# Two heads over two adjacent PSUM banks in one instruction, in the attention steps of a gated mix of two attention blocks

## The chip, the cores and the metric

One core of a Trainium2 chip runs the kernel as one program. The time is device microseconds of one launch. Three runs of the kernel before gave 2834.82 to 2836.29 us, median 2835.33. The engines are called PE (TensorE, matrix products), ACT (ScalarE, activations), DVE (VectorE, reductions and element-wise work), POOL (GpSimd) and SP (SyncE, which issues most DMAs). Each runs its own instructions in the order in which they were written, and semaphores order the engines among each other.

## The reference

Two multi-head attention blocks, A and B, each with its own weights, read the same input `x` of 2048 rows and 640 features (the reference gives `A_x` to both). Each has 32 heads of 20 features. A sigmoid gate of `x` mixes the two results row by row.

```python
q, k, v = qkv[0], qkv[1], qkv[2]
scores = jnp.einsum("bhqd,bhkd->bhqk", q, k) * scale
p = _softmax(scores, axis=-1)
o = jnp.einsum("bhqk,bhkd->bhqd", p, v)
...
g = _sigmoid((x * gate_w).sum(-1, keepdims=True))
return g * a + (1 - g) * b
```

The softmax subtracts the largest score of each row, so the kernel computes every score twice: once to find the row maxima, and once more, transposed and with the maximum already subtracted, to take the exponential.

## The kernel before

The 64 heads of both blocks are taken in 16 groups of four, and the 2048 queries in four blocks of 512. For each group and query block there are eight steps of 256 keys, 512 steps in all (`STEPS`). The main loop (L1103) walks through them, and one step holds four kinds of work on PE:

- **Scores** (`scores`, L624): for each of the two key tiles and each of the two head pairs, two matmuls, 128 keys by 512 queries. The two heads of a pair stand on the two halves of PE's rows, at 0 and 64, and can run at the same time. Each lands in a PSUM bank, and ACT takes its exponential into an SBUF tile `pt` (L635). That is eight a step.
- **Values** (`values`, L645): four matmuls per key tile, of the step before, which add to the one PSUM bank `acc`. PE shows eight matmul records for each such block.
- **Maxima** (`max_mm`, L558): the scores of later steps, 128 queries by 512 keys, about 15 steps ahead (`LEAD`). A unit has four chunks of 512 keys, taken in the order 0, 2, 1, 3 (`ORDER`), and two heads. Chunks 2 and 3 of both heads, and for most groups chunks 0 and 1 of the second head, go through a plain row maximum on DVE (L585). For the first head, chunk 0 holds the difference of two chunks' keys (`KD`); ACT takes its positive part into `rl` (L578), and DVE adds that to chunk 1 and takes the maximum in one instruction (L582). In group 0 both heads do so.
- **Blocks that fill** (`slot`, L1053): projections of queries, keys and values for later groups, and output products. One block is some 6 to 15 matmuls into one bank (`mms`, L368), which ACT or DVE then empties.

PSUM has eight banks: one is `acc`, and the other seven (`NB`) are single tiles that `take` (L122) hands out. It picks the bank that a small cost model of the engines thinks will come free first. `T_EXP`, `T_MAX` and the like are that model's costs; they only set which bank is picked. PE cannot write a bank before the instruction that reads it has ended.

The order of a step's work is written out by hand in `STEP` (L44). A letter stands for one call: `e0` and `e1` the score matmul of the one or the other head, `m0` and `m1` that of the maxima, `V` a block of value products, `X` a filling block. There are three orders: for a step with no filling block, with one, and with two; `LATE` is for the last steps, in which no maxima are left. Beside the `e` calls the loop moves smaller pieces along: `take_acc` (L732), which transposes `acc` on DVE once in eight steps (L736, L741, L747), and `finish_max` (L589), which gathers the maxima and sends them through DRAM into the rows of `QT`.

Of the kernel before, what the change touches and what calls it, by code (L numbers as in the profile page):

```python
# [19 lines left out]
P = 128  # L20
# [3 lines left out]
DH = 20  # L24
# [28 lines left out]
T_EXP, T_MAX, T_BACK = 0.478, 0.6, 0.15  # L53
REST = 6
# [7 lines left out]
def kernel(  # L62
# [18 lines left out]
    psum = ctx.enter_context(tc.tile_pool(name="psum", bufs=1, space=PSUM))  # L81
# [18 lines left out]
    acc = psum.tile([P, QB], F32, name="acc")  # L100
# [21 lines left out]
    def take():  # L122

        i = min((k for k in range(NB) if k not in held), key=lambda k: free_at[k])
        held.add(i)
        return i, banks[i]

# [32 lines left out]
    def scales(maxima, n, then):  # L160

        for _ in range(REST):
            yield
        yield PRODUCT
        i, pt = take()
        nc.tensor.transpose(pt[:n, :P], maxima[:, :n], ident)
        tick_block(0.1, free_at[i])
        yield
        e = wts.tile([5, 8], F32, name="e", tag="scl", bufs=2)
        nc.vector.tensor_reduce(e[:n, 0:1], pt[:n, :P], axis=AX.X, op=OP.max)  # L170
        give(i, spend("dve", 0.3, clock["done"]))
        spend("dve", 1.0)
        powers(e.bitcast(I32)[:n, :], 1)
        dg = wts.tile([5, 2, 5], F32, name="dg", tag="scd", bufs=2)
        for k in range(2):
            nc.vector.tensor_scalar(dg[:n, k, :n], ident[:n, :n], e[:n, 3 + k:4 + k], None, op0=OP.mult)
        for _ in range(REST):
            yield
        yield PRODUCT
        i, pb = take()  # L180
        tick_block(0.1, free_at[i])
        for k in range(2):
            nc.tensor.matmul(pb[:, k * n:(k + 1) * n], ones[:n, :], dg[:n, k, :n], start=True, stop=True)  # L183
        yield
        both = wts.tile([P, 10], F32, name="both", tag="scb", bufs=2)
        nc.vector.tensor_copy(both[:, :2 * n], pb[:, :2 * n])
        give(i, spend("dve", 0.2, clock["done"]))
        then(both[:, :n], both[:, n:2 * n])
# [179 lines left out]
    def mms(i, out_ap, pairs, cost):  # L368

        if now[0] >= 0:  # L370
            tick_block(len(pairs) * cost * T_SCORE, free_at[i])
        for k, (a, b) in enumerate(pairs):
            if now[0] < 0:
                tick_block(cost * T_SCORE, free_at[i])
            nc.tensor.matmul(out_ap, a, b, start=(k == 0), stop=(k == len(pairs) - 1))  # L375
            if now[0] < 0:
                yield
# [6 lines left out]
    def project_chunk(w, hi, lo, ch):  # L384

        wh, wl = w
        def pairs(n):
            if now[0] < 0:
                return ([(wh[:, c, :], b[:, c, n]) for c in range(NC) for b in (xh, xl)]
                        + [(wl[:, c, :], xh[:, c, n]) for c in range(NC)])  # L390
            return [(a[:, c, :], b[:, c, n]) for c in range(NC) for a, b in ((wh, xh), (wh, xl), (wl, xh))]

        t0 = ch * QB
        if now[0] >= 0:
            f = work.tile([P, QB], F32, name="fs")
            for k in range(3):
                if k:
                    yield
                m = slice(PARTS[k], PARTS[k + 1])
                i, pt = take()  # L400
                yield from mms(i, pt[:, m], pairs(slice(t0 + m.start, t0 + m.stop)), 0.34)
                nc.scalar.activation(f[:, m], pt[:, m], AF.Copy, scale=QKS)  # L402
# [116 lines left out]
    def project_v(gg, j):  # L519
# [3 lines left out]
        for u in range(2):  # L523
            if u and now[0] >= 0:
# [5 lines left out]
            nc.scalar.activation(V[gg % 2][:, j + u, :, 0:DH], pt[:, :160].rearrange("p (h d) -> p h d", h=2 * GH),  # L530
                                 AF.Copy, scale=QKS)
# [20 lines left out]
    relus, relu_at = {}, {}  # L552
# [5 lines left out]
    def max_mm(u, ch, heads=(0, 1)):  # L558
# [9 lines left out]
        for j in heads:  # L568
            two = u < NS or ch < 2 and (j == 0 or g == 0)
# [3 lines left out]
            k = KD[g % 2 if ch == 0 else 1][r, pair] if two and ch % 2 == 0 else KT[g % 2][r, pair, ch * QB:(ch + 1) * QB]  # L573
            nc.tensor.matmul(pt, QT[g % 2][r, pair, q0:q0 + P], k, start=True, stop=True)  # L574
            m = mparts[g, qb][:, pair, j, t, ch:ch + 1]
            if two and ch % 2 == 0:
                relus[u, j] = start.tile([P, QB], F32, name="rl0", bufs=4) if u < NS else work.tile([P, QB], F32, name="rl", bufs=2)
                nc.scalar.activation(relus[u, j], pt, AF.Relu)  # L578
                back = relu_at[u, j] = spend("act", T_EXP, ready)
            elif two:  # L580
                rl = relus.pop((u, j))
                nc.vector.tensor_tensor_reduce(rl, pt, rl, 1.0, LOW, OP.add, OP.max, m)  # L582
                back = spend("dve", T_MAX, max(ready, relu_at.pop((u, j))))
            else:
                nc.vector.tensor_reduce(m, pt, axis=AX.X, op=OP.max)  # L585
                back = spend("dve", T_MAX, ready)
            give(i, back)

# [35 lines left out]
    def scores(G, kk, pair, heads=(0, 1)):  # L624
# [3 lines left out]
        for j in heads:  # L628
            i, et = take()
            ready = tick_score(j, i)  # L630
            r = slice(64 * j, 64 * j + 64)
            nc.tensor.matmul(et, KT[g % 2][r, pair, kt * P:(kt + 1) * P],  # L632
                             QT[g % 2][r, pair, qb * QB:(qb + 1) * QB], start=True, stop=True)
            pt = pp.tile([P, QB], F32, name="pt")
            nc.scalar.activation(pt, et, AF.Exp, scale=factor(g // 4))  # L635
# [9 lines left out]
    def values(G, kk):  # L645
# [3 lines left out]
        for h in range(GH):  # L649
            nc.tensor.matmul(acc[32 * h:32 * h + VW, :], V[(g // 2) % 2][:, kt, (g % 2) * GH + h, :],  # L650
                             ptiles.pop((G, kk, h)), start=(kt == 0), stop=(kt == NT - 1))
# [33 lines left out]
    def out_tiles(job, t, state):  # L685
# [17 lines left out]
        def products():  # L703
            wh, wl = wo_parts[z]
            for k in range(0, D, width):
# [8 lines left out]
                if first:  # L714
                    nc.scalar.activation(y[:, n], pt[:, :width], AF.Copy, scale=f)
                else:
                    nc.vector.scalar_tensor_tensor(y[:, n], pt[:, :width], f, y[:, n], op0=OP.mult, op1=OP.add)
# [52 lines left out]
    def take_last():  # L770
# [5 lines left out]
        for t in range(4):  # L776
            nc.tensor.matmul(pt[:, 4 * t:4 * t + 4], ot[:, t * P:(t + 1) * P], one, start=True, stop=True)
        rc = work.tile([P, 16], F32, name="sq", bufs=2)
        nc.vector.reciprocal(rc, pt[:, :16])
        give(i, spend("dve", 0.3))  # L780
        i, pt = take()
        nc.tensor.transpose(pt[:16, :P], rc, ident)
        rt = wts.tile([16, P], F32, name="rt", tag="rt", bufs=1)
        nc.scalar.activation(rt, pt[:16, :P], AF.Copy)
        give(i, spend("act", 0.3))
        i, pt = take()
        for t in range(4):
            nc.tensor.matmul(pt[:, t * P:(t + 1) * P], picks[0].rearrange("p k e -> p (k e)")[:, t * P:(t + 1) * P], rt,
                             start=True, stop=True)
        o = work.tile([P, 2, QB], F16, name="on", bufs=2)  # L790
        for t in range(4):
            c = slice(t * P, (t + 1) * P)
            nc.vector.tensor_tensor(ot[:, c], ot[:, c], pt[:, c], op=OP.mult)
# [8 lines left out]
    def last_tiles(qb, o):  # L802
        wh, wl = wo_parts[2]
        for t in range(4):
            c = slice(t * P, (t + 1) * P)
            f = f_o[1][:, 4 * qb + t:4 * qb + t + 1]
            for half in range(2):
# [4 lines left out]
                for k, (a, w) in enumerate(((0, wh), (0, wl), (1, wh))):  # L812
                    nc.tensor.matmul(pt[:, :320], o[:, a, c], w[:, n], start=(k == 0), stop=(k == 2))  # L813
                if half and qb == NQ - 1 and t < 3:
                    part = pp.tile([P, QB], F32, name="pt")[:, :320]
                    nc.scalar.activation(part, pt[:, :320], AF.Copy, scale=f)
                    nc.gpsimd.tensor_tensor(y, y, part, op=OP.add)
                    give(i, spend("act", 0.42, clock["done"]))
                else:
                    nc.vector.scalar_tensor_tensor(y, pt[:, :320], f, y, op0=OP.mult, op1=OP.add)  # L820
# [35 lines left out]
    def turn(j0, c):  # L856
# [3 lines left out]
        for u in range(4):  # L860
            tick_block(0.11, free_at[i])
            nc.tensor.transpose(pt[:, u * P:(u + 1) * P], xs[:, j0 + u, c * P:(c + 1) * P], ident)  # L862
# [100 lines left out]
    start_stack.close()  # L963

    pp = ctx.enter_context(tc.tile_pool(name="pp", bufs=12))
# [119 lines left out]
    half_done = set()  # L1085

    def one_max(u, ch, j):
        max_mm(u, ch, (j,))
        if u % NS == NS - 1 and ch == ORDER[3]:
            if unit_of(u)[:2] in half_done:  # L1090
                finishing.append(unit_of(u)[:2])
            half_done.add(unit_of(u)[:2])
# [10 lines left out]
    for G in range(STEPS + 1):  # L1103
        g, qb, i = unit_of(G)
        now[0] = G
        while G < STEPS and ((g, qb) not in ready or (G and not valued(G - 1))):
            for u, ch in next_maxima(G, 1):
                for j in (1, 0):
                    one_max(u, ch, j)
# [7 lines left out]
        for what in (STEP[blocks] if maxima or some else LATE + " X" * (blocks == 2)).split():  # L1117
            k = count[what] = count.get(what, 0) + 1
            if what[0] == "e":
                q = sum(count.get(f"e{j}", 0) for j in range(2)) - 1  # L1120
                j = int(what[1])
                if G < STEPS:
                    scores(G, (k - 1) // 2, (k - 1) % 2, (j,))
                finish_step()
                advance()
                if q == 3:
# [3 lines left out]
            elif what[0] == "m":  # L1130
                for u, ch in some[(k - 1) * len(some) // 4:k * len(some) // 4]:
                    one_max(u, ch, int(what[1]))
# [44 lines left out]
```

## Time and profile before

| | |
|---|---|
| median of three runs | 2835.33 us |
| profiled execution, first to last instruction | 2832.8 us |
| mean granted TensorE clock | 0.996 |
| instructions | 62443 |
| PE matmuls | 23362 |
| HBM read, written | 48.89 MB, 26.61 MB |

The profile is of one execution. Its page gives the busy time of each engine, the chain of work that ended last, and the costliest groups of instructions; the timeline lists instructions in order of time, neighbours of one kind merged into one row with their count. A row of the timeline has the start, the length, the engine, the line, the operation, the tiles written and read, and in brackets the idle time just before it and who ended it. A row of a group has the count, then the busy time and the mean length of one in ns, then the idle time before them and who ended most of it. Matmul ends are modelled, so the start of the next matmul says more than the length of one. Times from the timeline are microseconds from the first instruction.

### The profile page before, as it was taken

To read this page: it belongs to the slowest core of one execution; us is meant where nothing else is said; L and a number is where in the kernel's file an instruction comes from. 1 tells how busy PE (TensorE), PEld (TensorE's weight loads), DVE (VectorE), ACT (ScalarE), POOL (GpSimd) and SP (SyncE) were. 2 spreads that over 40 slices of the span, in tenths; PEclk is the share of its full clock that TensorE was granted. 3 is DMA by queue.
4 is the path that set the end of the run, shared out by engine and by line. 5 is a ranking of instruction groups with operands and counts; after the bars stand their busy time and mean duration, and the time that the engine had idled before them with its cause. 6 is when DMAs were issued, how large, how long until landed. Compare 5 with 4: busy or idle time off the path is not lost.

```text
span 2832.8 us, 62443 instructions
## 1 busy us (share of the span) xinstructions
PE 2773.1 (98%) x23362; PEld 970.8 (34%) x23362; DVE 2443.8 (86%) x4763; ACT 2529.7 (89%) x5122; POOL 671.8 (24%) x914
## 2 busy tenths in 40 slices
PE   6999999999999999999999999999999999999998
PEld 3533223342323323343233333334333333332222
DVE  6688999879999898988989888887888989989982
ACT  3799999989999999989999999998899999888887
POOL 5312113231221212233431111222112233120011
PEclk9999999999999999999999999999999999999999
DMA  4110101001020101202021020211202112122222
GB/s 135 35 45 7 39 6 42 16 16 29 13 52 16 37 11 27 47 13 50 17 56 44 14 60 16 48 37 24 49 15 61 38 38 70 55 71 60 63 60 74
DMA packets 167170, 113.71 MB, mean 40 GB/s; under 512 B 102224, under 2 KB 140808, under 8 KB 166864
## 3 DMA queue, kind: packets, MB, share of 16 engines
q1 hardware_dynamic: 164320, 108.09, 15.6%
q8 instruction: 183, 3.00, 0.4%
q0 software_dynamic: 1600, 0.96, 0.2%
q14 instruction: 123, 1.01, 0.1%
q10 hardware_dynamic: 944, 0.66, 0.1%
HBM read 48.89 MB, written 26.61 MB: 27 GB/s over the span
## 4 chain that ended last, share of the span: by engine, by line
PE 91%; DVE 5%; ACT 1%; DMA 1%; POOL 1%; issue 1%; SPq 0%; POOLq 0%; DVEq 0%; ACTq 0%
PE acc L650 34%; PE bank L375 20%; PE bank L632 19%; PE bank L574 17%; DVE mpart L585 3%; ACT pt L635 1%; DVE rl L582 1%; DMA xs<-in_A_x_dram 0%; ACT rl L578 0%; DMA wv<-in_A_wqkv_dram 0%; DVE ot L736 0%; PE bank L813 0%; PE bank L183 0%; PE bank L862 0%; DVE wmax L227 0%
## 5 line engine op out<-in xcount | busy, mean ns | idle before, releaser
L635 ACT ACTIVATE pt<-bank 128x512 f32<-128x512 f32 x4096 | 2157.5, 614 | 155.0 <-PE bank L632 75.1
L585 DVE TENSOR_REDUCE mpart<-bank 128x1 f32<-128x512 f32 x2976 | 1867.8, 681 | 264.3 <-PE bank L574 167.1
L650 PE MATMUL acc<-pt,v 128*21 128x512 f32 x8192 | 1082.0, 600 | 3.4 <-DVE ot L736 3.1
L632 PE MATMUL bank<-qt,kt 64*128 64x512 f16 x4096 | 1056.3, 380 | 11.9 <-ACT pt L635 4.5
L574 PE MATMUL bank<-kt,qt 60*128 60x512 f16 x3536 | 1013.0, 380 | 4.0 <-DVE mpart L585 0.7
L574 PEld LDWEIGHTS <-qt 60*128 60x128 f16 x4096 | 235.4, 94 | 686.6 <-issue 629.0
L632 PEld LDWEIGHTS <-kt 64*128 64x128 f16 x4096 | 248.1, 94 | 456.7 <-issue 322.8
L582 DVE CUSTOM_DVE_ANT_0 rl<-bank,rl 128x512 f32<-128x512 f32 x560 | 377.5, 678 | 20.5 <-ACT rl L578 8.2
L578 ACT ACTIVATE rl<-bank 128x512 f32<-128x512 f32 x560 | 329.8, 595 | 14.6 <-PE bank L574 12.3
L744 POOL TENSOR_TENSOR ot<-ot,sq 128x512 f32<-128x512 f32 x63 | 66.0, 1047 | 993.0 <-DVE sq L741 993.0
L650 PEld LDWEIGHTS acc<-pt,v 128*21 128x21 f32 x8192 | 143.0, 99 | 434.6 <-issue 421.5
L375 PE MATMUL bank<-xx,wbh 128*128 128x168 f16 (+2 forms) x2240 | 280.1, 244 | 3.2 <-ACT xx L866 1.9
L375 PE MATMUL bank<-xx,wbl 128*128 128x168 f16 (+2 forms) x1120 | 252.8, 243 | 0.0
L375 PEld LDWEIGHTS <-wbh 128*128 128x128 f16 x2240 | 183.6, 98 | 86.8 <-issue 79.8
L574 PE MATMUL bank<-kd,qt 60*128 60x512 f16 x560 | 203.6, 381 | 1.7 <-DMA kd<-dd 1.2
L375 PE MATMUL bank<-wvh,xx 128*128 128x160 f16 (+1 forms) x1280 | 155.4, 234 | 0.5 <-ACT pt L635 0.3
L375 PE MATMUL bank<-woh,o_in 128*128 128x160 f16 (+1 forms) x960 | 155.7, 256 | 0.0
L375 PEld LDWEIGHTS <-xx 128*128 128x128 f16 x1920 | 131.6, 97 | 52.7 <-issue 49.4
L404 POOL CAST cq<-fs 128x512 f16<-128x512 f32 x60 | 36.6, 609 | 446.0 <-ACT fs L402 444.0
L375 PE MATMUL bank<-wvl,xx 128*128 128x160 f16 (+1 forms) x640 | 137.3, 231 | 0.6 <-POOL wvl L315 0.6
L375 PEld LDWEIGHTS <-o_in 128*128 128x128 f16 (+1 forms) x1440 | 104.0, 97 | 75.3 <-issue 62.2
L402 ACT ACTIVATE fs<-bank 128x168 f32<-128x168 f32 (+1 forms) x216 | 67.5, 313 | 56.6 <-PE bank L375 40.0
(131 smaller groups left out, 1305.2 us busy)
## 6 DMA issues: line engine op xcount, KB each, us to landing
y_scr<-y_out SPq DMA_DIRECT2D x32, 320.0 KB
kt<-cq SPq DMA_DIRECT2D x120, 80.0 KB
o_scr<-on SPq DMA_DIRECT2D x240, 40.0 KB
kt<-cq SPq DMA_DIRECT2D x136, 40.0 KB
xs<-in_A_x_dram SPq DMA_DIRECT2D x8, 640.0 KB
o_in<-o_scr SPq DMA_DIRECT2D x32, 160.0 KB
y_out<-y_scr SPq DMA_DIRECT2D x16, 320.0 KB
xx<-y_scr SPq DMA_DIRECT2D x16, 320.0 KB
```

Source lines behind the costliest of these rows:

```text
L375: nc.tensor.matmul(out_ap, a, b, start=(k == 0), stop=(k == len(pairs) - 1))
L402: nc.scalar.activation(f[:, m], pt[:, m], AF.Copy, scale=QKS)
L404: nc.gpsimd.tensor_copy(hi, f)
L574: nc.tensor.matmul(pt, QT[g % 2][r, pair, q0:q0 + P], k, start=True, stop=True)
L578: nc.scalar.activation(relus[u, j], pt, AF.Relu)
L582: nc.vector.tensor_tensor_reduce(rl, pt, rl, 1.0, LOW, OP.add, OP.max, m)
L585: nc.vector.tensor_reduce(m, pt, axis=AX.X, op=OP.max)
L632: nc.tensor.matmul(et, KT[g % 2][r, pair, kt * P:(kt + 1) * P], QT[g % 2][r, pair, qb * QB:(qb + 1) * QB], start=True, stop=True)
L635: nc.scalar.activation(pt, et, AF.Exp, scale=factor(g // 4))
L650: nc.tensor.matmul(acc[32 * h:32 * h + VW, :], V[(g // 2) % 2][:, kt, (g % 2) * GH + h, :], ptiles.pop((G, kk, h)), start=(kt == 0), stop= ...
L744: nc.gpsimd.tensor_tensor(t3, t3, sq.unsqueeze(2).to_broadcast([P, 16, 32]), op=OP.mult)
```

## The change

Scores and maxima now take two heads at a time. A new `take_two` picks two adjacent banks that are both free of the others' hands; the two matmuls of a pair go to one bank each, and one ACT instruction takes the exponential over both banks, 128 by 1024, into a tile `pt` of twice the width, of which there are six instead of twelve. For chunks 2 and 3 one DVE reduction over both banks gives both heads' maxima. In chunks 0 and 1 the plain maximum of the second head stays a single one (outside group 0), and so do the positive part and the fused instruction of the first; in group 0 the positive part covers both. The seven banks of the steps are one tile, so `matmul`, `transpose` and `read` declare which accesses don't depend on each other. The start of the kernel keeps single banks and `max_mm`. Each letter of `STEP` now stands for a pair: `E` for two score matmuls, `M` for two of the maxima, and the small pieces are moved along twice per `E`.

```diff
-STEP = ("e0 m1 V e1 m0 e0 m1 e1 m0 e0 m1 e1 m0 V e0 m1 e1 m0",
-        "X e0 m1 m0 e1 m0 m1 V m1 e0 e1 m0 e1 e0 V m0 e1 e0 m1",
-        "X m0 m1 e0 m1 e0 e1 V e1 e0 m1 m0 V e1 m0 m1 m0 e0 e1 X")
-LATE = "e0 e1 e0 e1 V X e0 e1 e0 e1 V"
+STEP = ("E M V E M E M V E M",
+        "X E M V E M E V M E M",
+        "X E M V E M X E M V E M")
+LATE = "E E V X E E V"
...
+T_EXP2, T_MAX2, T_TTR = 0.842, 1.133, 0.69
...
+    def take_two():
+
+        i = min((k for k in range(NB - 1) if k not in held and k + 1 not in held),
+                key=lambda k: (max(max(free_at[k:k + 2]), clock["pe"]), abs(free_at[k] - free_at[k + 1])))
+        held.update((i, i + 1))
+        return (i, i + 1), store[0][:, i:i + 2]
...
+    def apart(ins, keep):
+
+        for r, engine in recent:
+            if r not in keep and engine != ins.engine:
+                tc.declare_no_dep(ins, r, reason="a reader of another bank")
...
+    def max_two(u, ch):
...
+        n = two_heads(g, i) if ch < 2 else 0
+        ik, pt = take_two()
+        for j in range(2):
...
+            matmul(pt[:, j], QT[g % 2][r, pair, q0:q0 + P], k, start=True, stop=True)
+            ready = tick_score(j, ik[j])
...
+        if n < 2:
+            read(ik[n:], nc.vector.tensor_reduce(m[:, n:], pt[:, n:], axis=AX.X, op=OP.max))
+            back[n:] = [spend("dve", (T_MAX2, T_MAX)[n], ready)] * (2 - n)
+        for i, t in zip(ik, back):
+            give(i, t)
...
-        for j in heads:
-            i, et = take()
-            ready = tick_score(j, i)
+        ik, et = take_two()
+        for j in range(2):
             r = slice(64 * j, 64 * j + 64)
-            nc.tensor.matmul(et, KT[g % 2][r, pair, kt * P:(kt + 1) * P],
-                             QT[g % 2][r, pair, qb * QB:(qb + 1) * QB], start=True, stop=True)
-            pt = pp.tile([P, QB], F32, name="pt")
-            nc.scalar.activation(pt, et, AF.Exp, scale=factor(g // 4))
-            ptiles[G, kk, 2 * pair + j] = pt
-            weighed[G, kk] = spend("act", T_EXP, ready)
+            matmul(et[:, j], KT[g % 2][r, pair, kt * P:(kt + 1) * P],
+                   QT[g % 2][r, pair, qb * QB:(qb + 1) * QB], start=True, stop=True)
+            ready = tick_score(j, ik[j])
+        pt = pp.tile([P, 2, QB], F32, name="pt")
+        read(ik, nc.scalar.activation(pt, et, AF.Exp, scale=factor(g // 4)))
+        ptiles[G, kk, pair] = pt
+        weighed[G, kk] = spend("act", T_EXP2, ready)
+        for i in ik:
             give(i, weighed[G, kk])
...
+    store.append(psum.tile([P, NB, QB], F32, name="bank"))
+    banks[:] = [store[0][:, i] for i in range(NB)]
...
-    pp = ctx.enter_context(tc.tile_pool(name="pp", bufs=12))
+    pp = ctx.enter_context(tc.tile_pool(name="pp", bufs=6))
```

In the rows below `qt,kt` marks a score matmul (an `e`), `kt,qt` or `kd,qt` one of the maxima (an `m`), and `acc` a value product; in brackets is the engine whose reader PE waits for before it writes the bank. A number behind `bank` names one bank before the change; afterwards all seven are one tile.

The first place is PE at the end of a step with no filling block (step 111), up to and with its second block of value products. Before:

```order
L632 LDWEIGHTS kt_83
L632 MATMUL bank_93<-qt_81,kt_83 128x512 [waits DVE_49]
L574 LDWEIGHTS qt_81
L574 MATMUL bank_89<-kt_83,qt_81 128x512 [waits Activation_49]
L632 LDWEIGHTS kt_83
L632 MATMUL bank_94<-qt_81,kt_83 128x512 [waits DVE_49]
L574 LDWEIGHTS qt_81
L574 MATMUL bank_95<-kt_83,qt_81 128x512 [waits Activation_49]
L650 MATMUL acc<-pt,v_87 21x512 x4
```

and now:

```order
L159 LDWEIGHTS kt_86
L159 MATMUL bank<-qt_84,kt_86 128x512 [waits Activation_49]
L159 LDWEIGHTS kt_86
L159 MATMUL bank<-qt_84,kt_86 128x512 [waits DVE_49]
L159 LDWEIGHTS qt_84
L159 MATMUL bank<-kt_86,qt_84 128x512 [waits Activation_49]
L159 LDWEIGHTS qt_84
L159 MATMUL bank<-kt_86,qt_84 128x512
L736 MATMUL acc<-pt,v_90 21x512 x4
```

The heads of one kind stand next to each other. The last pair, of the maxima, waits once for both its banks, and what it waits for is the exponential over the pair that was written two pairs before it; that pair was the first behind the step's first block of value products.

The second place is PE in a step with one filling block (step 191), behind its second block of value products. Before:

```order
L574 LDWEIGHTS qt_80
L574 MATMUL bank_94<-kt_82,qt_80 128x512 [waits DVE_49]
L632 LDWEIGHTS kt_82
L632 MATMUL bank_95<-qt_80,kt_82 128x512 [waits Activation_49]
L632 LDWEIGHTS kt_82
L632 MATMUL bank_92<-qt_80,kt_82 128x512 [waits DVE_49]
L574 LDWEIGHTS qt_80
L574 MATMUL bank_93<-kt_82,qt_80 128x512 [waits Activation_49]
L375 LDWEIGHTS wbh
```

and now:

```order
L159 LDWEIGHTS qt_83
L159 MATMUL bank<-kt_85,qt_83 128x512 [waits Activation_49]
L159 LDWEIGHTS qt_83
L159 MATMUL bank<-kt_85,qt_83 128x512
L159 LDWEIGHTS kt_85
L159 MATMUL bank<-qt_83,kt_85 128x512 [waits DVE_49]
L159 LDWEIGHTS kt_85
L159 MATMUL bank<-qt_83,kt_85 128x512
L159 LDWEIGHTS qt_83
L159 MATMUL bank<-kt_85,qt_83 128x512 [waits Activation_49]
L159 LDWEIGHTS qt_83
L159 MATMUL bank<-kt_85,qt_83 128x512
```

Three pairs now stand between the second block of value products and the filling block, where there were two. Each has one wait, for the reader of the third pair before it.

More of the change, by code (lines that the diff above doesn't have):

```diff
@@ L126, in take, with on_bank, matmul, transpose @@
         return i, banks[i]
+    def take_two():
[3 more added lines that the diff above has]
+        return (i, i + 1), store[0][:, i:i + 2]
+    store, last_read = [], {}
+    fresh, recent = set(), []
+    def apart(ins, keep):
+        for r, engine in recent:
+            if r not in keep and engine != ins.engine:
+                tc.declare_no_dep(ins, r, reason="a reader of another bank")
+    def on_bank(out, ins, alone=True):
+        if store:
+            i = out.offset // QB
+            readers = last_read.get(i, [])
+            if alone:
+                apart(ins.ins, readers)
+            fresh.add(i)
+        return ins
+    def matmul(out, a, b, start=True, stop=True, alone=True):
+        return on_bank(out, nc.tensor.matmul(out, a, b, start=start, stop=stop), alone)
+    def transpose(out, a, alone=True):
+        return on_bank(out, nc.tensor.transpose(out, a, ident), alone)
+    def read(banks_read, ins, keep=(), alone=True):
+        name = ins.ins.name
+        if store:
+            for i in banks_read:
+                if i in fresh:
+                    fresh.discard(i)
+                    last_read[i] = []
+                last_read[i].append(name)
+            if alone:
+                apart(ins.ins, keep)
+            recent.append((name, ins.ins.engine))
+            del recent[:-24]
+        return name
     def spend(engine, cost, ready=0.0):
@@ L165, in scales @@
         i, pt = take()
-        nc.tensor.transpose(pt[:n, :P], maxima[:, :n], ident)
+        transpose(pt[:n, :P], maxima[:, :n])
         tick_block(0.1, free_at[i])
@@ L583, in max_mm, with two_heads @@
                 back = spend("dve", T_MAX, max(ready, relu_at.pop((u, j))))
-            else:
-                nc.vector.tensor_reduce(m, pt, axis=AX.X, op=OP.max)
-                back = spend("dve", T_MAX, ready)
             give(i, back)
+    def two_heads(g, i):
+        return 2 if g == 0 else 1
+    def max_two(u, ch):
+        g, qb, i = unit_of(u)
+        pair, t = divmod(i, 4)
+        if (g, qb) not in mparts:
+            max_parts(g, qb)
+        q0 = qb * QB + t * P
+        n = two_heads(g, i) if ch < 2 else 0
+        ik, pt = take_two()
+        for j in range(2):
+            r = slice(64 * j, 64 * j + 60)
+            k = (KD[g % 2 if ch == 0 else 1][r, pair] if j < n and ch % 2 == 0
+                 else KT[g % 2][r, pair, ch * QB:(ch + 1) * QB])
+            matmul(pt[:, j], QT[g % 2][r, pair, q0:q0 + P], k, start=True, stop=True)
+            ready = tick_score(j, ik[j])
+        m = mparts[g, qb][:, pair, :, t, ch]
+        back = [0.0, 0.0]
+        if n and ch % 2 == 0:
+            relus[u] = work.tile([P, 2, QB], F32, name="rl", bufs=1)
+            relu_by[u] = read(ik[:n], nc.scalar.activation(relus[u][:, :n], pt[:, :n], AF.Relu), keep=added)
+            back[:n] = [spend("act", T_EXP2 if n == 2 else T_EXP, ready)] * n
+            relu_at[u] = back[0]
+        elif n:
+            rl = relus.pop(u)
+            for j in range(n):
+                added.append(read([ik[j]], nc.vector.tensor_tensor_reduce(rl[:, j], pt[:, j], rl[:, j], 1.0, LOW, OP.add,
+                                                                          OP.max, m[:, j:j + 1]), keep=[relu_by[u]]))
+                back[j] = spend("dve", T_TTR, max(ready, relu_at[u]))
+            del added[:-4]
+        if n < 2:
[3 more added lines that the diff above has]
+            give(i, t)
     def finish_max(g, qb):
@@ L650, in values @@
             nc.tensor.matmul(acc[32 * h:32 * h + VW, :], V[(g // 2) % 2][:, kt, (g % 2) * GH + h, :],
-                             ptiles.pop((G, kk, h)), start=(kt == 0), stop=(kt == NT - 1))
+                             ptiles[G, kk, h // 2][:, h % 2], start=(kt == 0), stop=(kt == NT - 1))
+        for pair in range(2):
+            del ptiles[G, kk, pair]
     wo_parts = {}
@@ L1107 @@
             for u, ch in next_maxima(G, 1):
[L1108 to L1109 removed]
+                one_max(u, ch)
             finish_step()
```

88 lines of the change are left out of this document (44 added, 44 removed).

## The prediction

> **What bounds the kernel now.** I read the busy shares first, then the chain of waits, then the groups of instructions, then the timeline of single steps.
>
> ```profile
> span 2832.8 us, 62443 instructions
> PE 2773.1 (98%) x23362; PEld 970.8 (34%) x23362; DVE 2443.8 (86%) x4763; ACT 2529.7 (89%) x5122; POOL 671.8 (24%) x914
> PE 91%; DVE 5%; ACT 1%; DMA 1%; POOL 1%; issue 1%; SPq 0%; POOLq 0%; DVEq 0%; ACTq 0%
> L635 ACT ACTIVATE pt<-bank 128x512 f32<-128x512 f32 x4096 | 2157.5, 614 | 155.0 <-PE bank L632 75.1
> L585 DVE TENSOR_REDUCE mpart<-bank 128x1 f32<-128x512 f32 x2976 | 1867.8, 681 | 264.3 <-PE bank L574 167.1
> ```
>
> The chain that ended last is 91% PE, with ACT at 1%. The instructions that the change merges sit on ACT and DVE, which have 11 to 14% of the span idle. So the question is not what ACT saves but whether PE still runs without gaps. I write E for the two score matmuls of a head pair, M for the two of the maxima, V for one block of value products, X for a projection block, and M1 to M4 for the four M of a step. A step with one X looks like this on PE:
>
> ```profile
> 1105.92 0.32 PE L375 MATMUL bank<-xx,wbh 128*128 128x168 f16 x2
> ...
> 1107.11 0.39 PE L632 MATMUL bank<-qt,kt 64*128 64x512 f16 x1
> ...
> 1107.34 0.38 PE L574 MATMUL bank<-kd,qt 60*128 60x512 f16 x1
> ...
> 1107.87 1.06 PE L650 MATMUL acc<-pt,v 128*21 128x512 f32 x8
> ...
> 1108.86 0.39 PE L574 MATMUL bank<-kt,qt 60*128 60x512 f16 x1
> ...
> 1109.61 1.06 PE L650 MATMUL acc<-pt,v 128*21 128x512 f32 x8
> ...
> 1110.60 0.39 PE L574 MATMUL bank<-kt,qt 60*128 60x512 f16 x1
> ...
> 1111.14 0.32 PE L375 MATMUL bank<-xx,wbh 128*128 128x168 f16 x2
> ```
>
> X to X is 1111.14 - 1105.92 = 5.22 us with no idle entry on PE. Its parts: X 1.19; a slot of two matmuls on the two row halves 0.23 (1107.11 to 1107.34), 0.22 below; three slots up to a V 0.76 (1107.11 to 1107.87), so a change of kind costs about 0.09; V 0.99. Eight slots, two V, one X and three changes are the floor; the change alters none of these counts, so such a step cannot gain. A step without X is different (timeline again):
>
> ```profile
> 676.00 1.06 PE L650 MATMUL acc<-pt,v 128*21 128x512 f32 x8
> ...
> 713.66 1.06 PE L650 MATMUL acc<-pt,v 128*21 128x512 f32 x8
> ```
>
> and the busy times of PE, PEld, DVE, ACT and POOL in a window of such steps:
>
> ```profile
> 690.00:735.00 45.00, 43.93 (x309) 10.42 (x306) 43.44 (x82) 43.30 (x88) 8.32 (x13) 1.00 0.03 6
> ```
>
> Eight such steps lie between these two V, 37.66 us, 4.71 each. PE's work in one is 8 x 0.22 + 2 x 0.99 + 2 x 0.09 = 3.92; the window's row has DVE busy for 43.44 of 45.00 us and ACT for 43.30. Here, and only here, the two readers set the pace.
>
> **The change, part by part.** *The exponential.* 4096 become 2048 of twice the width. Its times in the timeline:
>
> ```profile
> 1000.21 0.60 ACT L635 ACTIVATE pt<-bank 128x512 f32<-128x512 f32 x1 [0.33 <-PE bank L574]
> ...
> 1000.86 0.37 PE L632 MATMUL bank<-qt,kt 64*128 64x512 f16 x1 [0.25 <-ACT pt L635]
> ...
> 1107.54 0.60 ACT L635 ACTIVATE pt<-bank 128x512 f32<-128x512 f32 x1
> ...
> 1109.31 3.04 ACT L635 ACTIVATE pt<-bank 128x512 f32<-128x512 f32 x6 [0.20 <-PE bank L632]
> ```
>
> and, from the groups by shape, the other widths that ACT reads:
>
> ```profile
> L402 ACT ACTIVATE fs<-bank 128x168 f32<-128x168 f32 x144 | 44.7, 310 | 31.0 <-PE bank L375 24.1
> L313 ACT ACTIVATE wvh<-wv,both 128x800 f16<-128x800 f32 x1 | 1.0, 952 | 0.0
> L313 ACT ACTIVATE wbh<-ws,both 128x400 f16<-128x400 f32 x1 | 0.6, 627 | 19.8 <-DVE both L186 19.8
> L313 ACT ACTIVATE wbh<-ws,both 128x240 f16<-128x240 f32 x1 | 0.5, 479 | 0.0
> L313 ACT ACTIVATE wvh<-wv,both 128x5 f16<-128x5 f32 x1 | 0.3, 306 | 0.0
> ```
>
> Matmul start to exponential start is 0.43 us (1107.11 to 1107.54); one lasts 0.60, back to back they come every (3.04 - 0.60) / 5 = 0.49, and PE writes the bank again 0.05 after the end (1000.81 to 1000.86). No row has 1024 elements. For 512 more, the two widest rows give (952 - 627) / 400 = 0.81 ns each, or 0.415 us, which I take: 1.02 us long, one every 0.905, PE back after 1.07. Bounds: the narrow rows' slope, (479 - 306) / 235 = 0.74 ns or 0.377 us, one every 0.87 and PE back after 1.03; and no saving at all, one every 0.98 and PE back after 1.14. Per step ACT saves 8 x 0.49 - 4 x 0.905 = 0.30 us, where X steps cannot use it.
>
> The row comes first: 614 ns at 512. "ScalarE: Activation LUTs" of the Trainium skill (What ACT_TABLE_LOAD costs) states 186 ns plus 0.833 ns an element, with 93 ns of overlap, and agrees with that row. By it the wide one is 1.04 us, one every 0.95, and the sum below would end near 3033 instead.
>
> *The plain maxima.* Pairs for two of the four M of a step; their reduce and the transposes beside them:
>
> ```profile
> L227 DVE TENSOR_REDUCE xm<-xs 128x1 f32<-128x1280 f32 x8 | 11.9, 1486 | 1.8 <-DMA xs<-in_A_x_dram 1.2
> L736 DVE STREAM_TRANSPOSE ot<-acc 128x512 f32<-128x512 f32 x63 | 44.9, 712 | 5.1 <-PE acc L650 2.7
> L747 DVE STREAM_TRANSPOSE ob<-ot 128x512 f32<-128x512 f32 x63 | 44.1, 700 | 0.0
> L741 DVE RECIPROCAL sq<-ot 128x16 f32<-128x16 f32 x63 | 16.0, 253 | 2.2
> ```
>
> and in the step shown above:
>
> ```profile
> 1107.57 2.48 DVE L585 TENSOR_REDUCE mpart<-bank 128x1 f32<-128x512 f32 x4 [0.48 <-PE bank L574]
> ...
> 1109.97 0.68 DVE L582 CUSTOM_DVE_ANT_0 rl<-bank,rl 128x512 f32<-128x512 f32 x1
> ...
> 1110.58 0.08 DVE L582 DVE_READ_ACCUMULATOR2_ANT mpart<- 128x1 f32 x1
> ```
>
> One reduce every (2.48 - 0.68) / 3 = 0.60; (1486 - 681) / 768 = 1.05 ns an element puts a wide one at 1.22 us, one every 1.14: 0.06 saved twice a step. With 0.69 for the fused add and maximum (1109.97 to 1110.66), M1 to M4 take 0.60 + 1.14 + 1.29 + 1.14 = 4.17 us of DVE, under any step time below.
>
> *The banks.* This is what costs. Seven banks held seven tiles in flight; in pairs they hold three and a spare. In the built order nearly every pair is rewritten at the third pair after it. So an M takes the pair of the last E but one, and waits for that whole exponential.
>
> *A step without X* (order E1 M1 V E2 M2 E3 M3 V E4 M4). M3 reuses E2's pair, and E2 is the first thing behind the V. From V's end: E2 at 0, exponential at 0.43, PE may write at 0.43 + 1.07 = 1.50, M3's slot and change 0.31, V 0.99: 2.80 us. The other half, V E4 M4 E1 M1 V, is the same loop: M1 waits for E4. PE has 1.95 us of work in each half and idles 0.85. The step takes 5.60 for 4.71. Queued behind the waiting M on PE is the V, and behind that the next E, so ACT starves in turn; its 0.30 us is lost there. The built order has 184 such halves, 92 steps: 92 x 0.89 = 82 us.
>
> *A step with one X* (X E1 M1 V E2 M2 E3 V M3 E4 M4). The second V stands ahead of M3, so E2's exponential (1.50) is done before M3's turn at 0.75 + 0.99 = 1.74. But M4 reuses E3's pair: E3's exponential starts at 0.43 + 0.905 = 1.335, PE may write at 2.405, and M4's turn is 1.74 + 0.44 = 2.18. PE waits 0.22. E4 needs M2's reduce: ready 0.65 + 1.22 + 0.05 = 1.92, turn 1.96, just hidden. M1 needs M3's banks, read from 2.17 to 3.46 and back at 3.6; its turn is after M4's (2.40 + 0.31) X and E1, at 4.1: hidden. The order has 318 such halves: 318 x 0.22 = 70 us. With the bounds (0.87 and 1.03, 0.98 and 1.14) the wait is 0.15 to 0.37, 48 to 118 us, and the loop above 2.76 to 2.87.
>
> *A step with two X.* They stood next to each other over the step's end and are now half a step apart:
>
> ```profile
> 589.87 0.32 PE L375 MATMUL bank<-xx,wbh 128*128 128x168 f16 x2
> 592.20 0.39 PE L574 MATMUL bank<-kd,qt 60*128 60x512 f16 x1
> ```
>
> Two in a row took 2.33; two single ones 2.38 and one change more, 0.09: 0.14 x 58 steps = 8 us. The X hides the exponentials there.
>
> *DVE's other work.* Once in eight steps a transpose and a reciprocal, 712 + 253 ns, stand between V and M3 on DVE. M1 has 0.5 us of room, so about 0.45 is exposed, in some 45 of the 63: 20 us; bounds 0 (the seven-bank order shows 5.1 us of idle there) and 40. I cost the steps without maxima at the end at nothing: a V or an X stands between their pairs and covers the exponential; uncovered, 16 steps at 0.3 would be 5 us.
>
> Sum on the profiled execution: 2833 + 82 + 70 + 8 + 20 = 3013; the median of the runs is 2.5 us above the span, so 3015.
>
> **Rivals.** *The X steps stay at their floor* because ACT or the row's slope is better than I take it: 2835 + 82 + 8 = 2925. For it: the wait is only 0.22 of 5.43 us. Against: no row allows a wide exponential under 0.87.
>
> *PE waits cascade*: each late M makes the next reduce late, so E4, with 0.04 us of room, waits too, and the spare bank's drain holds ACT. At 0.45 for each X half: 2835 + 82 + 143 + 8 + 40 = 3108. For it: the idle of DVE before a reduce is already 264.3 us with seven banks.
>
> *Faster*: in the steps without X the readers, and not the banks, keep setting the pace. DVE has 4.17 there and an eighth of 0.71 + 0.25 + 0.70 (the two transposes and the reciprocal), 4.38 for 4.71, X steps unchanged: 2835 - 92 x 0.33 + 8 = 2813. For it: DVE is 97% busy in that window. It decides if M3 may be written before E2's exponential ends, that is if the loop of 2.80 is under 2.19, for which the exponential would have to return its pair 0.46 us after its start, where a single one needs 0.65. Beside it stands "Advanced Engine Details and Errata" of the Trainium skill (TRN2 Errata), which advises tiles of 512 or 1024 elements to pay the gap between instructions less often; against it "Perfetto Trace Analysis" (Matmuls), that independent groups should rotate through the banks so that the reading of one overlaps the next. The trace sides with the second where PE is the chain.
>
> *The change doesn't do what it says*: all seven banks become one tile, and waits for readers of other banks come back. The order shows one wait a pair, mostly, so I count this with the cascade. *Nothing*: 2835.
>
> **How the numbers follow.** My sum 0.55, X at the floor 0.20, cascade 0.17, faster 0.05, nothing 0.03. A difference under 0.2% is what a measurement here cannot tell from none. Slower 0.92, same 0.03, faster 0.05. The range takes the floor case's lower side, 2910, to most of the cascade, 3095.
>
> **What would show it.** Steps without X near 5.6 us with PE idle about 0.85 twice, ended by the exponential, ahead of the second E or M of a V's half; X steps near 5.44 with one idle entry at M4, ended by the exponential; PE's share down to 93%, ACT's to about 78%. It is wrong if steps without X fall below 4.71, or if PE's idle ends on DVE.

## The result and the profile after

The changed kernel takes 3031.05 us (median of four runs, 3028.92 to 3031.89) against 2835.36 for the kernel before (2834.82 to 2836.29): 1.069 times as long, 95% interval 1.0675 to 1.0706. The prediction was 3015 us in a range of 2910 to 3095.

The page of the changed kernel, its span, busy shares, chain of waits and two of its groups:

```profile
span 3027.1 us, 59004 instructions
PE 2824.8 (93%) x23362; PEld 1040.9 (34%) x23362; DVE 2417.9 (80%) x3755; ACT 2443.9 (81%) x3050; POOL 670.7 (22%) x914
...
PE 80%; ACT 15%; DVE 2%; issue 2%; DMA 1%; POOL 1%; ACTq 0%; SPq 0%; DVEq 0%; POOLq 0%
...
L720 ACT ACTIVATE pt<-bank 128x1024 f32<-128x1024 f32 x2048 | 2035.6, 1022 | 333.6 <-PE bank L159 301.6
L159 PE MATMUL bank<-kt,qt 60*128 60x512 f16 x3536 | 771.8, 380 | 79.4 <-ACT pt L720 71.8
```

ACT and DVE have 3080 instructions fewer and are busy for 86 and 26 us less, and the span is 194 us longer. ACT, which was 1% of the chain, is 15% of it now. PE's waits, in total us, times and the longest, before and after:

```profile
PE bank L632 <- ACT pt L635: 4.5, 16, 0.5
```

```profile
PE bank L159 <- ACT pt L720: 144.8, 227, 1.1
```

A step without a filling block in the changed kernel's timeline, from its first V:

```profile
738.76 1.06 PE L736 MATMUL acc<-pt,v 128*21 128x512 f32 x8
...
739.75 0.39 PE L159 MATMUL bank<-qt,kt 64*128 64x512 f16 x2
...
740.18 1.94 ACT L720 ACTIVATE pt<-bank 128x1024 f32<-128x1024 f32 x2 [0.39 <-PE bank L159]
...
741.25 0.39 PE L159 MATMUL bank<-kt,qt 60*128 60x512 f16 x2 [0.68 <-ACT pt L720]
741.58 1.06 PE L736 MATMUL acc<-pt,v 128*21 128x512 f32 x8
...
742.57 0.39 PE L159 MATMUL bank<-qt,kt 64*128 64x512 f16 x2
...
743.06 1.94 ACT L720 ACTIVATE pt<-bank 128x1024 f32<-128x1024 f32 x2 [0.94 <-PE bank L159]
744.14 0.37 PE L159 MATMUL bank<-kd,qt 60*128 60x512 f16 x1 [0.75 <-ACT pt L720]
...
744.46 0.63 PE L736 MATMUL acc<-pt,v 128*21 128x512 f32 x4
```

This is the loop, twice: E behind the V at 739.75, its exponential from 740.18 to 741.20, the M that reuses its banks at 741.25 (an M and an E stand between the two), the next V at 741.58. ACT stands idle 0.94 us in the second half, because the E it needs is queued behind the V, and the V behind the waiting M. V to V is 2.82 and 2.88 us, 5.70 a step. A step with one X:

```profile
671.65 0.39 PE L159 MATMUL bank<-qt,kt 64*128 64x512 f16 x2
671.82 0.32 ACT L453 ACTIVATE fs<-bank 128x176 f32<-128x176 f32 x1 [0.43 <-PE bank L159]
...
672.18 1.02 ACT L720 ACTIVATE pt<-bank 128x1024 f32<-128x1024 f32 x1
672.19 1.06 PE L736 MATMUL acc<-pt,v 128*21 128x512 f32 x8
673.10 0.59 ACT L658 ACTIVATE rl<-bank 128x512 f32<-128x512 f32 x1
673.18 0.39 PE L159 MATMUL bank<-qt,kt 64*128 64x512 f16 x2
673.41 0.38 PE L159 MATMUL bank<-kt,qt 60*128 60x512 f16 x2
673.61 1.94 ACT L720 ACTIVATE pt<-bank 128x1024 f32<-128x1024 f32 x2
673.74 0.39 PE L159 MATMUL bank<-qt,kt 64*128 64x512 f16 x2
...
675.05 0.39 PE L159 MATMUL bank<-kt,qt 60*128 60x512 f16 x2
675.28 0.38 PE L159 MATMUL bank<-qt,kt 64*128 64x512 f16 x2
...
675.60 0.39 PE L159 MATMUL bank<-kt,qt 60*128 60x512 f16 x2
...
677.12 0.39 PE L159 MATMUL bank<-qt,kt 64*128 64x512 f16 x2
```

It takes 677.12 - 671.65 = 5.47 us for 5.22. Slots follow each other at 0.22 or 0.23 except at two places: E3 comes 0.33 behind M2 (673.41 to 673.74), when the positive part of M1 has ended (673.10 + 0.59 = 673.69); M4 comes 0.32 behind E4 (675.28 to 675.60), when the exponential of E3 has (the second of the two from 673.61 on, so 673.61 + 1.94 = 675.55). Neither has an idle entry, since PE's rows are modelled 0.38 long in a slot of 0.22.

The table gives the time from the first V of a step to that of the next in each profiled execution: the median over the steps with no block, with the 15 matmuls of one block, and with the 30 of two (76 to 98, 254 to 274, and 34 to 43 steps).

| kernel | time, us | no X | one X | two X |
|---|---|---|---|---|
| before | 2835.36 | 4.66 | 5.22 | 6.31 |
| the change | 3031.05 | 5.70 | 5.47 | 6.52 |
| v_order | 2982.43 | 5.16 | 5.47 | 6.52 |
| c_both_single | 2898.67 | 4.88 | 5.31 | 6.52 |
| b_max_single | 3100.35 | 5.54 | 5.54 | 6.57 |
| a_exp_single | 3191.47 | 5.77 | 5.94 | 6.57 |
| x_moved | 3002.10 | 5.16 | 5.38 | 6.57 |
| bo_pair_order | 2894.02 | 4.88 | 5.31 | 6.52 |
| d_exp_split | 3069.90 | 5.79 | 5.57 | 6.57 |
| e_red_split | 3043.93 | 5.75 | 5.49 | 6.52 |
| x_rotated | 3053.38 | 5.25 | 5.37 | 6.57 |
| f_both_split | 3083.11 | 5.84 | 5.60 | 6.57 |
| g_six_single | 3086.66 | 5.36 | 5.70 | 6.57 |

### The profile page after: what moved, and what is told of

Its sections match the earlier page's. It is cut to its first block, busy times and chain, and to the rows that moved or that the text cites. A ratio compares the mean times of both kernels' runs of the same rounds, so it can differ in the third digit from the quotient of the medians.

```text
span 3027.1 us, 59004 instructions
## 1 busy us (share of the span) xinstructions
PE 2824.8 (93%) x23362; PEld 1040.9 (34%) x23362; DVE 2417.9 (80%) x3755; ACT 2443.9 (81%) x3050; POOL 670.7 (22%) x914
## 4 chain that ended last, share of the span: by engine, by line
PE 80%; ACT 15%; DVE 2%; issue 2%; DMA 1%; POOL 1%; ACTq 0%; SPq 0%; DVEq 0%; POOLq 0%
PE bank L159 50%; PE acc L736 29%; ACT pt L720 13%; ACT rl L658 1%; DVE mpart L669 1%; DVE rl L664 1%; DMA xs<-in_A_x_dram 0%; DMA wv<-in_A_wqkv_dram 0%; PE bank L162 0%; ACT fs L453 0%; ACT v L581 0%; ACT y_out L803 0%; POOL wv L365 0%; ACTq L720 0%; POOL dd L516 0%
## 5 line engine op out<-in xcount | busy, mean ns | idle before, releaser
L720 ACT ACTIVATE pt<-bank 128x1024 f32<-128x1024 f32 x2048 | 2035.6, 1022 | 333.6 <-PE bank L159 301.6
L669 DVE TENSOR_REDUCE mpart<-bank 128x2 f32<-128x1024 f32 (+1 forms) x1968 | 1835.3, 958 | 308.9 <-PE bank L159 282.0
L159 PE MATMUL bank<-kt,qt 60*128 60x512 f16 x3536 | 771.8, 380 | 79.4 <-ACT pt L720 71.8
L159 PE MATMUL bank<-qt,kt 64*128 64x512 f16 x4096 | 814.3, 382 | 20.4 <-ACT pt L720 16.0
L664 DVE CUSTOM_DVE_ANT_0 rl<-bank,rl 128x512 f32<-128x512 f32 x528 | 360.7, 686 | 193.9 <-ACT pt L720 99.6
L159 PEld LDWEIGHTS <-qt 60*128 60x128 f16 x4096 | 263.6, 94 | 628.5 <-issue 593.7
L658 ACT ACTIVATE rl<-bank 128x512 f32<-128x512 f32 (+1 forms) x504 | 309.8, 615 | 1.1 <-DVE mpart L669 0.5
L159 PE MATMUL bank<-kd,qt 60*128 60x512 f16 x560 | 197.3, 377 | 59.8 <-ACT pt L720 57.1
```

Source lines behind the costliest of these rows:

```text
L159: return on_bank(out, nc.tensor.matmul(out, a, b, start=start, stop=stop), alone)
L658: relu_by[u] = read(ik[:n], nc.scalar.activation(relus[u][:, :n], pt[:, :n], AF.Relu), keep=added)
L664: added.append(read([ik[j]], nc.vector.tensor_tensor_reduce(rl[:, j], pt[:, j], rl[:, j], 1.0, LOW, OP.add, OP.max, m[:, j:j + 1]), keep=[ ...
L669: read(ik[n:], nc.vector.tensor_reduce(m[:, n:], pt[:, n:], axis=AX.X, op=OP.max))
L720: read(ik, nc.scalar.activation(pt, et, AF.Exp, scale=factor(g // 4)))
```

## The experiments

**v_order**: one V moved in the steps without X.

```diff
-STEP = ("E M V E M E M V E M",
+STEP = ("E M V E M E V M E M",
```

> The changed kernel with one edit: in steps without X the second V moves ahead of the third M (the order of a step with one X, without its X). My theory, that a step without X is a loop V, E, exponential, M that takes that E's banks, V: the M behind the second V finds the exponential done, and what is left is E1, which waits for M3's banks (read until 3.59 us after the first V's end), then M1 and V: 5.1 us a step for 5.70, 92 x 0.6 = 55 us less, about 2976 us in all, X steps unchanged at 5.47. Rival A, that the readers' own pace (a slower wide exponential or reduce) sets the step: 5.7 us and 3031. Rival B, that waits for readers of other banks cause it: 5.7 and 3031 too.

Measured: 2982.43 us, 48.6 less, and 5.16 us a step. No instruction became shorter; only a V stands where the exponential needs time. So the loop holds, and this run's rivals A (the readers' own pace) and B (waits for readers of other banks), which gave 3031, don't. What is left, in its timeline and in PE's waits:

```profile
736.43 1.02 ACT L720 ACTIVATE pt<-bank 128x1024 f32<-128x1024 f32 x1 [0.16 <-PE bank L159]
...
737.50 0.39 PE L159 MATMUL bank<-qt,kt 64*128 64x512 f16 x2 [0.80 <-ACT pt L720]
```

```profile
PE bank L159 <- ACT pt L720: 82.3, 109, 1.1
```

E1 waits for the exponential of E4 (736.43 + 1.02), and not for M3's reduce as I had expected: the picker gave E1 the pair two before.

**c_both_single**: the changed kernel with a bank and an instruction for each head, in pair order.

```diff
-        ik, et = take_two()
         for j in range(2):
...
-        read(ik, nc.scalar.activation(pt, et, AF.Exp, scale=factor(g // 4)))
+            i, et = take()
+            read([i], nc.scalar.activation(pt[:, j], et, AF.Exp, scale=factor(g // 4)))
```

(and in the same way for the maxima)

> The changed kernel with the pair order and the one tile for seven banks, but every score and maximum takes a bank of its own and has an instruction of its own, 512 wide. My theory (banks held in pairs cost): steps without X back at about 4.7 us, with one X at 5.22, two X at 6.45; total 2835 to 2850. Rival B (the order written in pairs, or waits that come from the one tile, cost): steps without X at 5.2 or more, total 2900 to 3030.

Measured: 2898.67 us. Two thirds of the loss go (132 of 196), but the floor isn't reached, and steps without X take 4.88. The figure lies between the two theories' ranges: banks in pairs are the larger part, and something of this run's rival B (the order in pairs, or the one tile) is there too.

**bo_pair_order**: the other half of that question, the kernel before with nothing but the pair order.

```diff
-STEP = ("e0 m1 V e1 m0 e0 m1 e1 m0 e0 m1 e1 m0 V e0 m1 e1 m0",
+STEP = ("e0 e1 m0 m1 V e0 e1 m0 m1 e0 e1 m0 m1 V e0 e1 m0 m1",
...
```

> The kernel before, with its seven separate single banks and its own calls, but the step orders of the changed kernel written out in single heads (e0 e1 for E, m0 m1 for M). If the order in pairs is what is left when banks are single again (2899 against 2835): 2885 to 2910, steps without X at 4.88 us and with one X at 5.31. If the one tile for seven banks and its declared dependencies are what is left: 2835 to 2850.

Measured: 2894.02 us, and the step times of c_both_single to 0.01 us. The order in pairs alone costs 59 us; what else c_both_single has of the change, the one tile with its declared dependencies among it, 4.7. By the table the order costs 0.22 us in a step without X, 0.09 with one and 0.21 with two; with the prediction's counts that is 92 x 0.22 + 318 x 0.09 + 58 x 0.21 = 61 us. Of this the prediction had only the last part, at 8 us.

**b_max_single and a_exp_single**: c_both_single's edit for the maxima alone, and for the exponentials alone.

> Exponentials over two banks stay; the maxima go back to one bank and one instruction each. My theory: an M no longer has to take a pair that an exponential has just held, if the picker gives it the three single banks, and ACT keeps its 0.3 us a step: steps without X 4.4 to 4.9 us, with one X 5.22 to 5.35, total 2810 to 2880. If the picker hands the exponentials' banks to the maxima, the late release of a wide exponential (1.07 us) still counts: total 2900 to 2960. Rival A (the wide exponential itself is the cost, wherever its banks go): 5.5 us and about 3000.

> The maxima of chunks 2 and 3 stay over two adjacent banks, and all maxima take banks in pairs; exponentials go back to one bank each. My theory: an M waits until two adjacent banks are free, but exponentials now free a bank every 0.49 us: steps without X 4.8 to 5.2 us, with one X 5.22 to 5.35, total 2850 to 2920. Rival A (the wide exponential is the cost): the time of before, 2835. Rival C (the wide reduce is the cost): near 3000.

Measured: 3100.35 and 3191.47 us; both missed, on the bad side. The changed kernel is no sum of a good and a bad half: pairs beside singles in seven banks are worse than pairs alone. The table shows where: in b_max_single the steps without X even got shorter (5.54 for 5.70), and the loss stands in those with one X, whose middle rose by only 0.07 but whose 90th percentile is 6.23 for 5.54. PE's waits in b_max_single changed hands:

```profile
PE bank L159 <- DVE mpart L668: 137.4, 260, 1.1
PE bank L159 <- ACT pt L721: 59.1, 94, 1.0
```

In its built order 1080 of the 2048 exponentials stand on two banks that one wide exponential had held before; the others wait for two readers. That broken pairs are the cause is argued from this and from e_red_split below, and not shown by a run that keeps them whole.

**d_exp_split, e_red_split, f_both_split**: the change's pairs of banks and order, but the wide exponential, the wide reduce, or both, as two instructions.

```diff
-        read(ik, nc.scalar.activation(pt, et, AF.Exp, scale=factor(g // 4)))
+        for j in range(2):
+            read([ik[j]], nc.scalar.activation(pt[:, j], et[:, j], AF.Exp, scale=factor(g // 4)))
```

> The changed kernel with its pairs of banks and its order, but each exponential in two instructions of 512. Tells what the merged instruction itself does. My theory: the pair comes back later, 1.57 us after its start for 1.50, and two in a row 2.55 for 2.41: steps without X 5.8, with one X 5.5 to 5.65, total 3045 to 3110; the merged instruction is a gain inside a loss. Rival A (the wide instruction is the cost): 2900 to 2990.

> The changed kernel with its pairs of banks and its order, but the maxima of chunks 2 and 3 in two reduces of 512, in the same pair of banks. My theory: DVE has room for the 0.06 us more twice a step, and the first bank is free 0.5 us sooner but the pair is not: 3025 to 3045. It also tells what made the kernel with maxima in single banks slow (3100): if narrow reduces do, this one is near 3100; if it is the pairs that single banks break up, it is near 3031. Rival C (the wide reduce is the cost): below 3000.

> The changed kernel with its pairs of banks and its order, but no wide instruction at all: two exponentials and two reduces where it has one. If the two merges act on their own, 3031 + 39 + 13 = 3083 (3070 to 3095); that less the time of the kernel with everything single (2899) is then the price of holding banks in pairs. If the pairs only cost because a wide reader returns both banks late: 2900 to 2990.

Measured: 3069.90, 3043.93 and 3083.11 us. Undoing a merge makes the kernel slower each time: the wide exponential is worth 39 us, the wide reduce 13, and both together 52 (3083.11 - 3031.05): they add up. So these runs' rivals A (the wide exponential is the cost) and C (the wide reduce is) fall. As two instructions the exponentials of a pair end later (601 ns each, one behind the other) than as one of 1022:

```profile
L721 ACT ACTIVATE pt<-bank 128x512 f32<-128x512 f32 x4096 | 2163.6, 601 | 263.0 <-PE bank L159 224.8
```

**g_six_single**: c_both_single with one of the seven banks out of use in the steps.

```diff
     banks[:] = [store[0][:, i] for i in range(NB)]
+    held.add(NB - 1)
```

> The kernel with the pair order and everything single (2899 us), with one of the seven banks taken out of use during the steps: six single banks, as many as three pairs hold, and the filling blocks have to share them. Tells whether pairs cost because one bank fewer is in use or because two banks come back at once. If the number of banks is what counts: near the 3083 of the kernel with pairs and narrow instructions (3050 to 3100). My theory, that it is the joint return (an M needs both banks of the exponentials just ahead of it): 2920 to 3010.

Measured: 3086.66 us, where I had expected 2920 to 3010: it lies in the range named for the case that the number of banks alone counts. The number of banks counts far more than I thought. The steps without X, where no block takes a bank, compare like with like: 4.88 us with seven single banks, 5.36 with six, 5.84 with three pairs (f_both_split, the same instructions). In these steps half of the price of pairs is the bank that cannot be paired, half the joint return. In steps with X the spare bank serves the blocks, while six singles have to serve them too, and the pairs are ahead (5.60 against 5.70); there the two halves are not told apart.

**x_moved and x_rotated**: v_order, with X moved ahead of M4; then with the picker replaced by a fixed rotation. Both have the moved V of v_order; the rotation also sends single tiles to the seventh bank first.

```diff
-        "X E M V E M E V M E M",
+        "E M V E M E V M E X M",
```

> The kernel with the moved V (2982 us), and in steps with one X the X also moves, from the step's start to just ahead of M4. My theory, that an X step loses 0.25 us at two waits of PE, 0.11 for the positive part of M1 ahead of E3 and 0.10 for the exponential of E3 ahead of M4: the X gives E3's exponential 1.2 us, so M4's wait goes; 5.25 to 5.37 us for 5.47, total 2915 to 2950. Rival B (the order in pairs makes PE's own slots dearer): X steps stay at 5.47 and the total at 2982.

> The kernel with V and X moved (3002 us, where I had expected 2915 to 2950), with a fixed rotation in place of the picker: pairs take banks 0-1, 2-3, 4-5 in turn, single tiles take bank 6 first. My theory, that the picker spoiled the moved X by giving pairs the banks of the pair two before (then a wait of E for the exponential just ahead of it): every pair is rewritten at the third after it, and steps with one X reach 5.25 to 5.37 us, total 2920 to 2950. If the waits of the moved X come from elsewhere: 5.38 us or more in the middle and 2980 to 3010 in all.

Measured: 3002.10 and 3053.38 us, both slower than v_order; both expectations missed. The middle of the X steps did fall, to 5.38 and 5.37, but a good part of them got longer, to 5.88 at the 90th percentile in both, against 5.52 before the move. The rotation did what it should to the exponentials, for which PE waited 117.4 us in x_moved; PE's waits in x_rotated:

```profile
PE bank L160 <- DVE mpart L670: 48.3, 169, 1.8
PE bank L160 <- DVE mpart L665: 43.3, 113, 1.0
PE bank L160 <- DVE xx L910: 17.0, 17, 1.3
...
PE bank L160 <- ACT pt L721: 14.4, 24, 1.1
PE bank L160 <- DVE both L238: 11.0, 8, 1.7
PE bank L160 <- DVE e L222: 10.3, 7, 1.5
```

With X in front of them, M4 and M1 reach DVE together, and E3 now waits for M1's reduce, here with its second matmul:

```profile
675.69 1.23 DVE L670 TENSOR_REDUCE mpart<-bank 128x2 f32<-128x1024 f32 x1 [0.37 <-PE bank L160]
...
678.12 0.37 PE L160 MATMUL bank<-qt,kt 64*128 64x512 f16 x1 [0.18 <-DVE mpart L670]
```

The rotation left the steps with one X at 5.37 and 5.88, so the picker alone was not what spoiled the move there: the wait goes from one reader to the other. The 51 us that x_rotated takes more than x_moved are another matter: 38 us of its waits (17.0, 11.0 and 10.3) are for readers of single tiles, which x_moved hardly shows (0.4). So crowding the single tiles into one bank is a large part of that difference, and its total is no measure of the rotation of pairs.

## Why the prediction was right

The likeliest case came true, and the mechanism with it in the steps without X: three pairs in flight, the loop V, E, exponential, M, with PE idle ahead of the M. In the X steps only half of the wait stood where it was forecast. The terms on the profiled execution, predicted and measured:

- **Steps without X**: 5.60 predicted, 5.70 measured; 82 us, and 92 x (5.70 - 4.71) = 91. The loop was 2.82 and 2.88 for 2.80; the second E's exponential began 0.49 behind its matmuls and not 0.43. The rows show 0.68 and 0.75 of PE's idle for the 0.85 forecast; the modelled row ahead of it is 0.16 longer than its slot (0.38 for 0.22), and with that they are 0.84 and 0.91.
- **Steps with one X**: 5.44 predicted, 5.47 measured; 70 us, and 318 x 0.25 = 80. Here the size came out, but at the wrong place, and that it came out is luck. I had the whole 0.22 at M4. It is 0.10 there and 0.11 at E3: the drain of X stands ahead of E1's exponential on ACT (671.82 to 672.14), which starts at 672.18 instead of 671.65 + 0.43 = 672.08, so the positive part of M1 ends late. I had followed M1's and M3's reduces and not the positive part.
- **Steps with two X**: 0.14 predicted, 0.21 measured (6.52 - 6.31); 8 us, and 12.
- **DVE's transposes**: 20 us predicted, -4 measured. The steps with one X that hold them grew by less than the others, 0.16 against 0.24, so with the prediction's count 45 x (0.16 - 0.24) = -4 us. The kernel before already paid for them (5.37 for 5.19), the changed one pays less (5.53 for 5.47). The term took the whole of its cost for new.
- **Not costed**: steps with value projections, 5.61 for 5.36, 28 of them after, 7 us.

Together 186 of 194 us, where the prediction had 180. One term was 24 us too large and the others together 30 too small; that this nearly cancels is luck too.

The wide exponential was 1022 ns for 1.02 predicted, one every 1.94 - 1.02 = 0.92 for 0.905. The formula of "ScalarE: Activation LUTs" (What ACT_TABLE_LOAD costs) of the Trainium skill gives 1.04, 2% more than the row. The 3033 that the prediction gives by that formula leaves out the longer exponential at M4; its own steps come to about 3040. The wide reduce was 1.22 as predicted:

```profile
L669 DVE TENSOR_REDUCE mpart<-bank 128x2 f32<-128x1024 f32 x1008 | 1229.9, 1220 | 281.4 <-PE bank L159 261.9
```

One reason was incomplete. I put nearly the whole loss on banks in pairs. The runs split it: 59 us for the order in pairs, 5 for the one tile and what goes with it, 184 for banks in pairs (3083.11 - 2898.67), and 52 gained by the wide instructions: 59 + 5 + 184 - 52 = 196. These are differences along one line of versions, so they add up by construction, and the mixed versions show that edits do not simply add. All but 8 us of the order's cost was in no term; which wait causes it is not shown here. Nor is nearly every pair rewritten at the third after it, as the prediction has it: in the built order 3141 of 4064 are, and 426 E take the pair of the E two before, as E1 does in v_order.

PE's share fell to 93% as forecast, ACT's to 81% (78% forecast); the idle entry forecast at M4 does not exist, since a wait of 0.10 us leaves none.

Of the rivals, X steps at their floor is ruled out by the 5.47, and so is the cascade, which needed 5.67; the faster case is ruled out by the loop itself, and with single banks the one tile costs no more than the 5 us above.

"Advanced Engine Details and Errata" of the Trainium skill (TRN2 Errata) advises large tiles to pay less often for the gap between instructions. These runs agree: the wide instructions gained 52 us. "Perfetto Trace Analysis" of the Trainium skill (Matmuls) says that independent groups should rotate through different banks, so that one is read while the next is computed; it does not say through how many. Here three pairs in place of seven single banks cost 184 us.

No version beat the kernel before; the best, bo_pair_order, is 2.1% slower (1.0191 to 1.0225).

## What to carry to other kernels

A merged instruction saves overhead on its own engine (worth 52 us here), and pays with buffers (184 us here): whatever it reads is taken and given back as one. Before merging, count the tiles in flight afterwards, and follow the loop from a slot of the producing engine through the reader back to the slot that reuses the bank, with every long block that stands in the same queue between them. If the producing engine is the chain, the saving on a reader counts only as far as that reader stands in the loop, and what the loop takes beyond the producing engine's own work is lost time.

## What was not expected of the hardware

- PE's waits of about 0.1 us leave no idle entry. The two of an X step, 0.21 us or 67 us over the 318 places, are seen only from start to start (0.32 and 0.33 for 0.22); PE's busy time rose from 2773.1 to 2824.8 us with the same 23362 matmuls.
- One PSUM bank of seven is worth 188 us here (3086.66 - 2898.67), 6.5% of the time.
